# A planner rule that lets the attention's small tiled products of blocks 3 to 5 wait for company, and starts every block's attention 2 plan units earlier

## Chip, cores and metric

The kernel runs on one core of a Trainium2 chip. The metric is the device time in microseconds; before the change it is 610.1 us, the median of three runs (608.67 to 610.43).

## The reference, cut to what matters

A recurrent attention (state of 48 x 48 for each of 4 x 8 heads, 768 steps), then a dense layer of width 2048 with a gated activation, then a soft mixture of experts:

```python
cur = np.einsum('bhd,bhe->bhde', u[None] * kt, vt)
y[:, :, t] = np.einsum('bhd,bhde->bhe', rt, state + cur)
state = wt[:, :, :, None] * state + np.einsum('bhd,bhe->bhde', kt, vt)
...
h = x @ w_in
g = h * (1.0 / (1.0 + np.exp(-1.702 * h)))
return (g @ w_out).astype(np.float32)
...
slot_input = d.T @ x
h = np.maximum(slot_input[e] @ w1[e], 0.0)
return (c @ slot_out).astype(np.float32)
```

Here `d` and `c` are softmaxes of `x @ phi` over the tokens and over the slots.

## The kernel before

The 3072 tokens are cut into six blocks of 512 (128 time steps of each of the four batches). A block's attention is done in four units, one for a batch: units 0 to 3 belong to block 0, units 12 to 15 to block 3, units 20 to 23 to block 5. Block by block the dense layer and the first part of the mixture follow; the experts and the output come at the end.

One unit has these steps. VectorE scans the decays and scales `at` (L595, L609, L617). TensorE makes the products of keys and receptances inside a chunk of 64 steps into `aps` (L657; 16 small products of a 48-row by 64-column tile; the program's step `ta`). VectorE masks them into `st` (L669). TensorE then does two half units into `y` (L709 and L711, 64- and 48-column tiles over 112 or 128 rows; steps `h0` and `h1`). VectorE rescales the state after each (L716 into `vs`), adds the two parts (L719 into `nat`), TensorE transposes the result (L725 into `xps`), and ScalarE and VectorE split it into a high and a low part (`xth` L736, `xtl` L739). From block 2 on VectorE also transposes the keys (L694 to L698), in blocks 0 and 1 TensorE does it (L662).

The dense layer of a block takes 16 slices `f` of its width. For each, nine products of a full 128x128 array give `h` (L810), ScalarE applies the activation twice (`gh` L814, `g` L818), VectorE subtracts (`gl` L822), and nine more full products go into the three banks of `x2` (L830 to L832). Block 1 is done in two halves of 256 columns, the other blocks with 512. The mixture's share of a block is `lg` (L910), `ln` (L925), `en` (L954) and `pp` (L962) on TensorE, with 16 transposes into `x2g` on VectorE (L898) in blocks 1 to 3 and a copy `es` (L957). The raw weights of slice `f` come in by DMA (`raw`, L498) and are converted during block 0.

All of this is one list of steps. `Plan.order` plays it through with assumed costs, engine by engine: of the steps that are ready, the one with the lowest priority number goes next. The priority of a unit of block u is `begin(u) - AHEAD` plus a small step, so that attention of a block lies beside the dense layer of the block before it; that of slice `f` grows through the block's period of 82. The order that comes out is written down and each engine runs its own list strictly in that order.

A *small product* below is one of L657, L709 or L711 (and L910 and L962, which also use a part of the array's columns); a *stretch* is a run of small products with no full product between.

Of the kernel before, what the change touches and what calls it, by code (L numbers as in the profile page):

```python
# [52 lines left out]

SOON = "w0 r0 n0 w1 r1 v0 n1 v1 w2 r2 c0 n2 v2 w3 r3 c1 n3 v3 c2 c3"

FIRST, SECOND, PERIOD, LAG, AHEAD = 30.0, 150.0, 82.0, 4.2, 74.0
CONV0, CONVD, CONVL = 6.0, 4.0, 16.0
ATT0, ATTD = 3.0, 3.0
LAT = {"PE": 0.3, "ACT": 0.25, "DVE": 0.2, "POOL": 0.2, "DMA": 2.2, "X": 0.0}
SAME = {"PE": 0.0, "ACT": 0.2, "DVE": 0.12, "POOL": 0.1, "DMA": 2.2, "X": 0.0}  # L60
FROM = {"PE": 1.9, "ACT": 2.0, "DVE": 1.0, "POOL": 1.0, "DMA": 0.9}
MM = 0.238


def act(n):
# [3 lines left out]
def dve(n, rate=960):  # L69
    return 0.16 + n / rate  # L70
# [6 lines left out]
class Plan:  # L77
# [6 lines left out]

    def __init__(self, caps):
        self.caps, self.steps, self.users, self.tag = dict(caps), [], {}, {}

    def add(self, eng, cost, fn, need=(), pr=0.0, take=(), use=(), port=False):
        n = len(self.steps)
        opts = dict(eng) if isinstance(eng, dict) else {eng: cost}  # L90
        for tag, key in take:
            self.tag.setdefault(key, []).append(tag)
        keys = list(dict.fromkeys([k for _, k in take] + list(use)))
        for k in keys:
            self.users[k] = self.users.get(k, 0) + 1
        self.steps.append((opts, isinstance(eng, dict), fn, [x for x in need if x is not None], pr, [t for t, _ in take], keys, port))
        return n

    def order(self):
        steps, caps, left = self.steps, dict(self.caps), dict(self.users)  # L100
        wait = [len(s[3]) for s in steps]
        out = [[] for _ in steps]
        for i, s in enumerate(steps):
            for d in s[3]:
                out[d].append(i)
        ready, free, port = {}, {}, 0.0
        for s in steps:
            for e in s[0]:
                free[e] = FROM.get(e, 0.0)
                ready.setdefault(e, [])  # L110
        at, on = [0.0] * len(steps), [None] * len(steps)

        def enter(i):
            for e in steps[i][0]:
                ready[e].append(i)

        for i, s in enumerate(steps):
            if not wait[i]:
                enter(i)
        events, now, got = [(t, -1, -1) for t in sorted(FROM.values())], 0.0, []  # L120
        seq = 0
        self.log = []
        while len(got) < len(steps):
            moved = False
            for e in ready:
                if free[e] > now + 1e-9:
                    continue
                best = None
                for i in ready[e]:
                    s = steps[i]  # L130
                    if at[i] > now + 1e-9 or any(caps[t] < s[5].count(t) for t in s[5]):
                        continue
                    if (e == "POOL" or e == "DVE" and s[7]) and port > now + 1e-9:
                        continue
                    if best is None or (s[4], i) < (steps[best][4], best):
                        best = i
                if best is None:
                    continue
                s = steps[best]
                for x in s[0]:  # L140
                    ready[x].remove(best)
                on[best] = e
                for t in s[5]:
                    caps[t] -= 1
                got.append((best, e))
                self.log.append((now, s[0][e]))
                free[e] = now + s[0][e]
                if e == "POOL" or e == "DVE" and s[7]:
                    port = free[e]
                heapq.heappush(events, (free[e], seq, best))  # L150
                heapq.heappush(events, (free[e] + LAT[e], seq + 1, -1))
                seq += 2
                moved = True
            if moved:
                continue
            if not events:
                raise RuntimeError(f"plan stuck at {now}: {[(e, len(r)) for e, r in ready.items()]} {caps}")
            now, _, i = heapq.heappop(events)
            done = [i] if i >= 0 else []
            while events and events[0][0] <= now + 1e-9:  # L160
                k = heapq.heappop(events)[2]
                if k >= 0:
                    done.append(k)
            for i in done:
                e = on[i]
                for k in steps[i][6]:
                    left[k] -= 1
                    if not left[k]:
                        for t in self.tag.get(k, ()):
                            caps[t] += 1  # L170
                for j in out[i]:
                    wait[j] -= 1
                    at[j] = max(at[j], now + (SAME[e] if list(steps[j][0]) == [e] else LAT[e]))
                    heapq.heappush(events, (at[j], seq, -1))
                    seq += 1
                    if not wait[j]:
                        enter(j)
        self.span = now
        return got
# [185 lines left out]
def rwkv_moe_softmoe_kernel(tc: tile.TileContext, ark, aw, nat, vr, ub, wf, phi, w1, w2, r, k, v, w, ug, out):  # L365
# [16 lines left out]
    plan = Plan({"ps": 8, "h": 2, "a": 3, "g": 1, "gh": 2, "at": 2, "aw": 2, "nat": 2, "st": 2, "fl": 3, "q": 2,  # L382
                 "xt": 2, "xl": 2, "ind": 1, "raw": RAWB, "cq": CQB, "w": NF, "ew": NEW, "gl": 2})
# [167 lines left out]
    def unit_nodes(i):  # L551
        u, b = order[i]
# [11 lines left out]
        def pr(k):  # L564
            return base + step * k
# [134 lines left out]
        def half(p):  # L700
            vl, vh = VROW[p]
            ol, oh = RNG[p]
            yps = t_[ky0] if p else bank(ky0)
            sps = bank(ky1) if p and u < NU - 1 else yps
            k1 = (ROWS if u else CH) if p == 0 else P
            for h in range(NH):
                cols = slice(h * DH, (h + 1) * DH)
                rhs = v[0:k1, p, cols]
                pe.matmul(yps[vl:vh, cols], S[0][0:k1, p, h, 0:CH], rhs, start=True, stop=True)  # L709
                if p == 0 or u < NU - 1:  # L710
                    pe.matmul(sps[ol:oh, cols], S[0][0:k1, p, h, CH:ROWS], rhs, start=True, stop=True)  # L711
# [34 lines left out]
        few = u < UQ  # L746
        ln = N("DMA", 0.55 if few else 1.64, ld_n, pr=soon(f"n{i}", pr(1) - 5), take=[("nat", n_)])
        def psum(key):
            return [("ps", key), ("a", key)]
# [14 lines left out]
        ta = N("PE", 0.8 if four else 1.08, pa, [a1, r0], pr(2), take=[x for k in kap for x in psum(k)], use=[a_])  # L764
# [14 lines left out]
        h0 = N("PE", 1.06, lambda: half(0), [k0, rc[0], lv, h.get("s1")] + ke0, pr(4), take=psum(ky0), use=[s_])  # L779
        s0 = N("DVE", dve(DM), lambda: snew(0), [h0, h.get("h1")], pr(5), use=[ky0, f_])  # L780
        h1 = N("PE", 1.06, lambda: half(1), [s0, k1, rc[1], lv] + ke1 + (nst if u == 0 else []), pr(6), take=psum(ky1) if not last else [], use=[s_, ky0])
# [3 lines left out]
        xh = N("ACT", act(DM), xhi, [tx], pr(9), take=[("xt", kx), ("xl", kx)] if b == 0 else [], use=[kxp, kx])  # L785
        xl = N("DVE", dve(DM), xlo, [xh], pr(9), use=[kxp, kx])
        hist[i] = {"h0": h0, "h1": h1, "s1": s1}
        xt_ready[i] = xl
        att_all.extend([y1, xl] + ([s1] if s1 is not None else []))

# [3 lines left out]
    def mm_nodes(blk, f, lo, wd):  # L794
# [4 lines left out]
        cols = slice(lo, lo + wd)  # L799
        mm = MM * (wd + 18) / (T + 18)  # L800

# [209 lines left out]
    for u in range(NU):  # L1011
        for b in range(NB):
            unit_nodes(NB * u + b)
        for lo in range(0, T, WIDE[u]):
            for f in range(NF):
                mm_nodes(u, f, lo, WIDE[u])
        moe2_nodes(u)
# [189 lines left out]
    for i, wd in enumerate(PIECES):  # L1207
# [5 lines left out]
        for g in range(2):  # L1213
# [18 lines left out]
            for p in range(4):  # L1232
                keys = list(dict.fromkeys(f"w2_{a // (4 * DM)}" for a in at0[8 * p:8 * p + 8]))
                at = p0 + 0.5 + p if i and g else p0 - 1 + g + 0.1 * p
# [120 lines left out]
```

## Time and profile before

| what | value |
|---|---|
| median of three runs | 610.1 us (608.67 to 610.43) |
| the profiled execution | 612.51 us, of which the span of the instructions is 610.6 us |
| TensorE matmul busy | 571.3 us (94%) |
| VectorE busy | 446.8 us (73%) |
| ScalarE busy | 274.2 us (45%) |
| GpSimd busy | 57.5 us (9%) |
| full products of the dense layer, L810 and L830 to L832 | 204.8 + 121.6 and 124.9 + 120.9 + 120.8 us |
| small products L709, L711, L657 | 60.2, 49.1 and 23.0 us |

Busy times overlap on TensorE, since matmuls are pipelined and their ends are modelled; what a product costs is read from the distance between two starts.

### The profile page before, as it was taken

The numbers are of one execution on the slowest core, as the hardware profiler recorded it, in microseconds if no ns is written. First come the engines' busy times: TensorE is split into PE (matmuls) and PEld (weight loads), VectorE is DVE, ScalarE is ACT, GpSimd is POOL, SyncE is SP. The second block draws the span as 40 slices with busy tenths as digits, with TensorE's granted clock in tenths as the row PEclk, the third lists the DMA queues.
The fourth block names the chain that finished last, engine by engine and source line by source line (L and its number), as shares of the span: only waits on it lengthen the run. The fifth ranks groups of instructions, "written<-read, shape, count | busy, mean of one in ns | idle before, by whom it ended". The sixth has DMA issues, their size and how long they took to land.

```text
span 610.6 us, 12651 instructions
## 1 busy us (share of the span) xinstructions
PE 571.3 (94%) x5196; PEld 462.4 (76%) x5196; DVE 446.8 (73%) x867; ACT 274.2 (45%) x532; POOL 57.5 (9%) x67
## 2 busy tenths in 40 slices
PE   1977999999999999999999999999999999998992
PEld 1846788878899998778777778777788778886371
DVE  7698899998988898998989997699872342113221
ACT  3474687748634345344435242353342353324131
POOL 2000000000130111022111202110310000000000
PEclk9995899999999999999999999999999999999897
DMA  8946554724623233033421223230110296558738
GB/s 223 311 143 180 196 154 139 245 81 123 179 82 117 79 111 111 22 105 110 120 82 64 87 83 103 86 111 25 51 40 1 95 380 203 196 181 289 264 113 254
DMA packets 30276, 84.53 MB, mean 138 GB/s; under 512 B 3840, under 2 KB 13696, under 8 KB 30208
## 3 DMA queue, kind: packets, MB, share of 16 engines
q1 hardware_dynamic: 28624, 82.84, 42.2%
q8 instruction: 43, 0.70, 0.5%
q10 hardware_dynamic: 1584, 0.79, 0.5%
q14 instruction: 25, 0.20, 0.1%
HBM read 78.89 MB, written 4.72 MB: 137 GB/s over the span
## 4 chain that ended last, share of the span: by engine, by line
PE 80%; DVE 10%; DMA 5%; ACT 2%; issue 1%; SPq 0%; DVEq 0%; ACTq 0%
PE h L810 30%; PE x L830 11%; PE x L831 10%; PE x L832 10%; PE y L709 5%; DMA raw<-in_wf_dram 3%; DVE x2g L898 3%; PE aps L657 2%; DMA aw<-in_aw_dram 2%; PE eh L1180 2%; PE y L711 2%; PE so L1222 2%; PE xps L725 1%; PE fo L1263 1%; DVE at L617 1%
## 5 line engine op out<-in xcount | busy, mean ns | idle before, releaser
L810 PE MATMUL h<-xth,w 128*128 128x512 f32 (+1 forms) x672 | 204.8, 369 | 0.7 <-ACT xth L736 0.6
L814 ACT ACTIVATE ghgh<-h 128x512 fp32r<-128x512 f32 (+1 forms) x112 | 59.9, 535 | 196.5 <-PE h L810 152.7
L810 PEld LDWEIGHTS h<-xth,w 128*128 128x128 f32 x672 | 122.5, 190 | 21.5 <-ACT xth L736 1.2
L830 PE MATMUL x<-ghgh,w 128*128 128x512 f32 (+1 forms) x336 | 124.9, 372 | 0.0
L810 PE MATMUL h<-xtl,w 128*128 128x512 f32 (+1 forms) x336 | 121.6, 362 | 0.4 <-DVE xtl L739 0.4
L831 PE MATMUL x<-glgh,w 128*128 128x512 f32 (+1 forms) x336 | 120.9, 360 | 0.0
L832 PE MATMUL x<-ghgh,w 128*128 128x512 f32 (+1 forms) x336 | 120.8, 360 | 0.0
L822 DVE TENSOR_TENSOR glgh<-g,ghgh 128x512 fp32r<-128x512 f32 (+1 forms) x112 | 71.6, 639 | 59.0 <-ACT g L818 57.6
L830 PEld LDWEIGHTS x<-ghgh,w 128*128 128x128 f32 x336 | 63.4, 189 | 11.8 <-issue 1.7
L810 PEld LDWEIGHTS h<-xtl,w 128*128 128x128 f32 x336 | 63.9, 190 | 9.3 <-DVE xtl L739 1.1
L832 PEld LDWEIGHTS x<-ghgh,w 128*128 128x128 f32 x336 | 63.4, 189 | 9.6
L831 PEld LDWEIGHTS x<-glgh,w 128*128 128x128 f32 x336 | 63.5, 189 | 9.2 <-DVE glgh L822 0.4
L709 PEld LDWEIGHTS y<-vs,st 128*64 128x64 f32 (+2 forms) x768 | 53.4, 148 | 16.5 <-issue 8.0
L818 ACT ACTIVATE g<-h 128x512 f32<-128x512 f32 (+1 forms) x112 | 59.6, 532 | 9.0 <-DVE glgh L822 8.6
L709 PE MATMUL y<-vs,st 128*64 128x48 f32 (+2 forms) x768 | 60.2, 235 | 2.8 <-DVE vs L716 2.0
L711 PE MATMUL y<-vs,st 128*48 128x48 f32 (+2 forms) x704 | 49.1, 226 | 0.9 <-ACT st L679 0.8
L711 PEld LDWEIGHTS y<-vs,st 128*48 128x48 f32 (+2 forms) x704 | 43.1, 130 | 1.4 <-ACT st L679 1.2
L716 DVE TENSOR_TENSOR vs<-y,fl 48x384 f32<-48x384 f32 x44 | 24.5, 556 | 22.2 <-PE y L711 21.5
L669 DVE TENSOR_TENSOR st<-aps,mask 64x256 f32<-64x256 f32 (+1 forms) x80 | 37.9, 474 | 3.4 <-PE aps L657 2.0
L621 ACT ACTIVATE st<-at 48x512 f32<-48x512 f32 x44 | 27.6, 627 | 25.1 <-DVE at L617 13.4
L657 PE MATMUL aps<-at 48*64 48x64 f32 x768 | 23.0, 235 | 14.7 <-DVE at L617 14.7
L657 PEld LDWEIGHTS aps<-at 48*64 48x64 f32 x768 | 19.5, 145 | 21.0 <-DVE at L617 15.4
(159 smaller groups left out, 694.4 us busy)
## 6 DMA issues: line engine op xcount, KB each, us to landing
w<-in_w_dram SPq DMA_DIRECT2D x32, 768.0 KB, 6.0
at<-in_ark_dram SPq DMA_DIRECT2D x24, 512.0 KB, 4.2
raw<-in_wf_dram SPq DMA_DIRECT2D x16, 768.0 KB, 4.8
nat<-in_nat_dram SPq DMA_DIRECT2D x20, 576.0 KB, 3.7
aw<-in_aw_dram SPq DMA_DIRECT2D x24, 448.0 KB, 4.1
vs<-in_vr_dram SPq DMA_DIRECT2D x48, 96.0 KB, 2.5
out_dram<-ot SPq DMA_DIRECT2D x6, 512.0 KB, 6.8
nat<-in_nat_dram SPq DMA_DIRECT2D x4, 192.0 KB, 4.9
```

The source lines that it names most:

```text
L621: ac.activation(S[0][lo:hi, p, :, 0:CH], t_[a_][lo:hi, 0], AF.Copy)
L657: pe.matmul(ab[p if four else 0][vl:vh, col:col + CH], t_[a_][lo:hi, 1, 4 * g + h], t_[a_][lo:hi, 0, 4 * g + h], start=True, stop=True)
L669: ve.tensor_tensor(S[0][vl:vh, p, n * g:n * g + n, 0:CH], t_[kap[p if four else 0]][al:ah, 0:n * CH].rearrange("p (h t) -> p h t", h=n), m ...
L709: pe.matmul(yps[vl:vh, cols], S[0][0:k1, p, h, 0:CH], rhs, start=True, stop=True)
L711: pe.matmul(sps[ol:oh, cols], S[0][0:k1, p, h, CH:ROWS], rhs, start=True, stop=True)
L810: pe.matmul(h[:, :wd], a, b, start=(k == 0), stop=(k == len(seq) - 1))
L814: ac.activation(t_[kgh][0], t_[kh][:, :wd], AF.Gelu_apprx_sigmoid)
L818: ac.activation(t_[kg], t_[kh][:, :wd], AF.Gelu_apprx_sigmoid)
L822: ve.tensor_tensor(gl, t_[kg], gh.bitcast(F32), op=ALU.subtract)
L830: pe.matmul(o, whi, gh, start=(f == 0), stop=False)
L831: pe.matmul(o, whi, gl, start=False, stop=False)
L832: pe.matmul(o, wlo, gh, start=False, stop=(f == NF - 1))
```

## The change

`AHEAD` goes from 74 to 76, which moves the priority of every unit from block 1 on. The steps `ta`, `h0` and `h1` of blocks 3 to 5 (units 12 to 23) are put into a set `tiled`. When the planner picks TensorE's next step, such a step gets 50 off its priority number if the step just placed was of the set too; otherwise, if fewer than two of the ready steps are of the set, it gets 500 on top until it has been ready for 8 plan units. The planner also adds 0.2 to its own cost of a step of the set that follows one outside it. No step is added or removed.

```diff
-FIRST, SECOND, PERIOD, LAG, AHEAD = 30.0, 150.0, 82.0, 4.2, 74.0
+FIRST, SECOND, PERIOD, LAG, AHEAD = 30.0, 150.0, 82.0, 4.2, 76.0
...
+SWITCH, HOLD, GROUP = 0.2, 8.0, 2
...
+                    can.append(i)
+                few = sum(i in self.tiled for i in can) < 2
+                rank = {i: steps[i][4] for i in can}
+                for i in can if e == "PE" else []:
+                    if i in self.tiled:
+                        rank[i] += -50.0 if tiled else 500.0 if few and now < at[i] + HOLD else 0.0
+                for i in can:
+                    s = steps[i]
...
-                    if best is None or (s[4], i) < (steps[best][4], best):
+                    if best is None or (rank[i], i) < (rank[best], best):
...
+                if e == "PE":
+                    free[e] += SWITCH if best in self.tiled and not tiled else 0.0
+                    tiled = best in self.tiled
...
+        if u > GROUP:
+            plan.tiled.update((ta, h0, h1))
```

In the changed program line numbers are 14 higher from the planner on, and 16 higher from the dense layer on.

**TensorE at the turn from block 3 to block 4.** `y0_19`/`y1_19` is unit 19's second half unit (its last row here), `aps20` and `y0_20` are unit 20's, `h4_0` opens block 4. Before:

```order
L711 MATMUL y1_19_4516<-vs3_95,st1_97 48x48
L810 MATMUL h3_15_0_4533<-xth3_3110,w15_1215 128x512
...
L725 MATMUL xps19_4548<-ident_78,nat19_4171 128x128 x3
L657 MATMUL aps20_0_4557<-at20_4231 64x64
...
L810 MATMUL h4_0_0_4584<-xth4_3995,w0_237 128x512
```

With the change:

```order
L725 MATMUL y0_19_4464<-vs3_95,st1_97 48x48
L671 MATMUL aps20_0_4481<-at20_4137 64x64
...
L846 MATMUL x2_3_0_3841<-ghgh3_13_0_4448,w13_1095 128x512
...
L725 MATMUL y1_19_4525<-vs3_95,st1_97 48x48
L723 MATMUL y0_20_4547<-vs0_92,st0_96 64x48
...
L826 MATMUL h3_15_0_4568<-xth3_3189,w15_1209 128x512
...
L739 MATMUL xps19_4581<-ident_78,nat19_4217 128x128 x3
L846 MATMUL x2_3_0_3841<-ghgh3_14_0_4542,w14_1149 128x512
...
L846 MATMUL x2_3_0_3841<-ghgh3_15_0_4585,w15_1209 128x512
...
L826 MATMUL h4_0_0_4631<-xth4_3923,w0_237 128x512
```

Unit 20's `aps` now stands right behind unit 19's first half, its first half right behind unit 19's second, and between the transposes of unit 19 and block 4's first product there are two groups of full products (and unit 20's second half) where there was only `aps20`.

**VectorE behind unit 9's second half unit**, in the second half of block 1 (the first row of each reads `y1_9`). Before:

```order
L716 TENSOR_TENSOR vs1_93<-y1_9_2199,fl9_1977 48x384
L822 TENSOR_TENSOR glgh1_15_0_2191<-g1_15_0_2197,ghgh1_15_0_2190 128x256
L719 TENSOR_TENSOR nat9_1798<-y0_9_2149,nat9_1798 128x384
L609 SCALAR_TENSOR_TENSOR aw10_1761<-aw10_1761,ind_91 112x512
L822 TENSOR_TENSOR glgh1_0_256_2232<-g1_0_256_2245,ghgh1_0_256_2231 128x256
L617 TENSOR_TENSOR at10_1836<-at10_1836,aw10_1761 112x1024
L739 TENSOR_TENSOR xtl2_1960<-xps9_2248,xth2_1959 128x3x128
L822 TENSOR_TENSOR glgh1_1_256_2267<-g1_1_256_2279,ghgh1_1_256_2266 128x256
L694 STREAM_TRANSPOSE st0_96<-at10_1836 32x8x32 x2
```

With the change:

```order
L733 TENSOR_TENSOR nat9_1778<-y0_9_2146,nat9_1778 128x384
L623 SCALAR_TENSOR_TENSOR aw10_1845<-aw10_1845,ind_91 112x512
L608 MEMSET ind_91 112x8
L609 SCALAR_TENSOR_TENSOR aw11_2093<-aw11_2093,ind_91 112x512
L838 TENSOR_TENSOR glgh1_0_256_2247<-g1_0_256_2264,ghgh1_0_256_2246 128x256
L753 TENSOR_TENSOR xtl2_2054<-xps9_2242,xth2_2053 128x3x128
L631 TENSOR_TENSOR at10_1891<-at10_1891,aw10_1845 112x1024
L614 TENSOR_TENSOR fl11_2308<-aw11_2093 112x8
L708 STREAM_TRANSPOSE st0_96<-at10_1891 32x8x32 x2
L710 STREAM_TRANSPOSE st0_96<-at10_1891 32x8x32 x2
L708 STREAM_TRANSPOSE st0_96<-at10_1891 32x8x32 x2
L838 TENSOR_TENSOR glgh1_1_256_2277<-g1_1_256_2280,ghgh1_1_256_2276 128x256
```

The subtraction `gl` of slice 1 now stands behind a scan of unit 11 and six transposes of unit 10 that came after it or elsewhere before; the `gl` of slice 15 no longer stands in this piece.

**SyncE's DMA issues in block 0.** `vs0` is the load of unit 8's values, which waits for both half units of unit 4. Before:

```order
L498 DMA raw13_1036<-in_wf_dram 128x2x768
L572 DMA aw7_1056<-in_aw_dram 112x1024
L498 DMA raw14_1112<-in_wf_dram 128x2x768
L589 DMA vs0_92<-in_vr_dram 64x384
L590 DMA vs0_92<-in_vr_dram 64x384
L498 DMA raw15_1166<-in_wf_dram 128x2x768
```

With the change:

```order
L512 DMA raw13_1043<-in_wf_dram 128x2x768
L603 DMA vs0_92<-in_vr_dram 64x384
L604 DMA vs0_92<-in_vr_dram 64x384
L512 DMA raw14_1110<-in_wf_dram 128x2x768
L586 DMA aw7_1134<-in_aw_dram 112x1024
L512 DMA raw15_1153<-in_wf_dram 128x2x768
```

The load of the values moved ahead of that of the weights of slice 14, and `aw7` behind it.

## Rows read from the trace of the kernel before

**Rows 1.** The page's busy times, and VectorE's busy tenths in 40 slices of the span.
```profile
PE 571.3 (94%) x5196; PEld 462.4 (76%) x5196; DVE 446.8 (73%) x867; ACT 274.2 (45%) x532; POOL 57.5 (9%) x67
DVE  7698899998988898998989997699872342113221
```

**Rows 2.** The page's chain by engine; pieces of the chain: start us, us, what.
```profile
PE 80%; DVE 10%; DMA 5%; ACT 2%; issue 1%; SPq 0%; DVEq 0%; ACTq 0%
177.41 1.08 PE h L810 x9
...
200.48 0.62 PE aps L657 x32
...
509.61 2.04 PE h L810 x9
```

**Rows 3.** Timeline of TensorE: start us, us, engine line op names shapes xcount [idle before <-releaser].
```profile
335.74 0.39 PE L832 MATMUL x<-ghgh,w 128*128 128x512 f32 x1
336.06 0.26 PE L709 MATMUL y<-vs,st 112*64 112x48 f32 x1
...
336.91 0.28 PE L709 MATMUL y<-vs,st 112*64 112x48 f32 x2
337.12 0.50 PE L830 MATMUL x<-ghgh,w 128*128 128x512 f32 x1
337.46 0.39 PE L831 MATMUL x<-glgh,w 128*128 128x512 f32 x1
...
339.39 0.26 PE L709 MATMUL y<-vs,st 128*64 128x48 f32 x1
```

**Rows 4.** Timeline of TensorE: `aps` followed by `y` and by a transpose.
```profile
109.41 1.15 PE L657 MATMUL aps<-at 48*64 48x64 f32 x32
110.48 0.26 PE L709 MATMUL y<-vs,st 112*64 112x48 f32 x1
...
137.31 1.15 PE L657 MATMUL aps<-at 48*64 48x64 f32 x32
138.39 0.60 PE L662 MATMUL kps<-ident,at 112*128 112x112 f32 x4
```

**Rows 5.** Timeline of TensorE: waits at three turns of blocks.
```profile
155.00 0.85 PE L962 MATMUL pp<-x2g,es 128*32 128x385 f32 x8 [0.52 <-DVE es L957]
...
333.01 0.85 PE L962 MATMUL pp<-x2g,es 128*32 128x385 f32 x8 [0.29 <-DVE x2g L898]
...
398.93 0.49 PE L725 MATMUL xps<-ident,nat 128*128 128x128 f32 x3
399.35 0.69 PE L657 MATMUL aps<-at 48*64 48x64 f32 x32
400.15 0.49 PE L810 MATMUL h<-xth,w 128*128 128x512 f32 x1
401.03 0.50 PE L810 MATMUL h<-xtl,w 128*128 128x512 f32 x1 [0.38 <-DVE xtl L739]
```

**Rows 6.** Timeline of VectorE: behind unit 9, and single rows of other stretches.
```profile
192.46 0.55 DVE L716 TENSOR_TENSOR vs<-y,fl 48x384 f32<-48x384 f32 x1 [1.48 <-PE y L711]
193.04 0.42 DVE L822 TENSOR_TENSOR glgh<-g,ghgh 128x256 fp32r<-128x256 f32 x1
...
196.90 0.42 DVE L822 TENSOR_TENSOR glgh<-g,ghgh 128x256 fp32r<-128x256 f32 x1
197.35 0.88 DVE L694 STREAM_TRANSPOSE st<-at 32x256 f32<-32x256 f32 x2
...
382.49 0.16 DVE L600 TENSOR_TENSOR fl<-aw 112x8 f32<-112x8 f32 x1
...
399.20 0.07 DVE L594 MEMSET ind<- 112x8 f32 x1
399.30 1.22 DVE L595 TENSOR_TENSOR_SCAN aw<-aw,ind 112x512 f32<-112x512 f32 x1
...
404.28 2.00 DVE L617 TENSOR_TENSOR at<-at,aw 112x1024 f32<-112x1024 f32 x1
```

More of the change, by code (lines that the diff above doesn't have):

```diff
@@ L86, in __init__ @@
         self.caps, self.steps, self.users, self.tag = dict(caps), [], {}, {}
+        self.tiled = set()
     def add(self, eng, cost, fn, need=(), pr=0.0, take=(), use=(), port=False):
@@ L121, in order @@
         seq = 0
-        self.log = []
+        self.log, tiled = [], False
         while len(got) < len(steps):
@@ L127, in order @@
                     continue
-                best = None
+                best, can = None, []
                 for i in ready[e]:
```

## Prediction

> **What bounds the kernel now.** I read the busy times and the chain first. TensorE is busy 94% of the span, and the chain of waits that ends last runs through it for 80%, through VectorE for 10% [rows 1, 2]. VectorE's slices stand at 8 and 9 tenths for the first two thirds of the span and then fall to 1 to 4 [rows 1]. So TensorE sets the pace, and until about 420 us VectorE is close enough behind to make it wait at single points. What this change can bring is therefore of two kinds: time that TensorE loses at each turn between full and small products, and waits on VectorE that come or go.
>
> The price of a turn is in the timeline [rows 3]. Nine full products of 512 columns take 2.04 us [rows 2], 0.23 a product. The first product of a half unit starts 0.32 us after the last full one instead of 0.23: 0.09 to go in. Inside, starts follow each other every 0.03 us (31st at 336.91, first at 336.06), although 64- and 48-column tiles alternate; from the 32nd to the next full product it is about 0.15, so 0.12 more to get out. The second full product then comes 0.34 after the first instead of 0.23, and the group of nine that lies between two half units takes 337.12 to 339.39, 2.27 instead of 2.04: without the 0.09 of the next entry that is 0.14 to get going again. One stretch of small products costs 0.09 + 0.12 + 0.14 = 0.35 us beyond its own work.
>
> **The change, part by part.** No product is added or taken away, so everything lies in the order.
>
> *Fewer stretches.* I counted them in the two orders, from block 1's first `aps` to block 5's first product; before and behind that, TensorE's order is the same. Before there are 64 stretches, with the change 56. Before, 4 neighbours are of unlike shape (`aps5` ahead of a half unit, and three `pp` ahead of one). With the change 12 are neighbours: 4 times a half unit follows another (units 15/16, 17/18, 19/20, 21/22), 6 times `aps` follows a half unit, and once each `lg` and `pp` lie beside one.
> - Two half units side by side: the trace has no such pair at full speed. Bounds: 0.23, if the way out is paid between them all the same, and 0.35, if nothing is. Since no break shows inside a half unit where its tiles alternate [rows 3], I take 0.35: 4 x 0.35 = 1.40 us.
> - Unlike shapes side by side: `aps` takes 1.08 us up to the start of a half unit and 1.08 up to a transpose that uses the whole width [rows 4]. The way out is paid whatever follows; entry and restart, 0.09 + 0.14 = 0.23, are saved. Bounds: nothing, and the whole 0.35. With 0.23, 8 new ones less the 4 given up give 4 x 0.23 = 0.92.
>
> Together 2.3 us. The Trainium skill, page "TensorEngine Tiling (Array Packing)", section "Tiling Modes", says that changing the tiling mode, and not just the tile, drains TensorE. That speaks against the six places where `aps` (48 rows) follows a half unit (112 or 128 rows), since the mode changes there as well. If each change cost half of the 0.35, an unlike pair would save 0.18 and the sum would be 1.40 + 4 x 0.18 = 2.1 us; the rows on `aps` agree that the drain stays.
>
> *Waits that go.* Three waits of TensorE on VectorE stand at turns of blocks [rows 5]. At 400.15 block 4's first product begins 1.2 us after unit 19's transposes, and its second, which reads `xtl`, comes 0.88 later instead of 0.34: 0.54 lost. The new order puts two groups of full products and a half unit there, over 5 us. `pp` of block 0 waits 0.52 for `es`, because it stood straight behind `en`; now a group of nine of 256 columns and a third of another lie between, 1.4 us [rows 2]. `pp` of block 2 waits 0.29 for the last `x2g` transpose; it gets one more group of nine ahead of it, 2.04. Sum 1.35 us, with nothing of it left if the VectorE work ahead is on time there.
>
> *A wait that comes.* The 2 units of `AHEAD` pull unit 11's scan ahead of a subtraction that TensorE needs in block 1. Before, VectorE's piece from the rescaling behind unit 9 to the `gl` of slice 1 ran from 192.46 to 197.32, 4.86 us without a gap [rows 6]. Now it lacks one narrow `gl` (0.35 after overlap) and holds also a memset and a scan (1.24), `fl` (0.1) and three pairs of transposes (0.88 each, 2.65): 8.5 us, from 0.1 after unit 9's second half. TensorE, in that time, has six narrow groups of 1.08 [rows 2], the restart 0.14, three transposes at about 0.3 (0.42 where a small product comes next [rows 5]), the entry 0.09 and `aps10` at 0.62 [rows 2]: 7.6. The second product of the next group, 0.12 on, reads `gl`. So TensorE waits 8.6 - 7.7 = 0.9 us. Lower bound 0, if VectorE gets there early. Upper bound: `at`'s scaling took 2.00 in one place instead of about 1.2 [rows 6]; if that 0.8 fell on all three long operations of the piece, 0.9 + 2.4 = 3.3.
>
> *What is moved at no cost.* A half unit held back for up to 8 plan units delays its unit, but the next user of its state is the same batch's unit one block on; what needs it soonest is the first product of the next block. There unit 23's transposes have one group of nine ahead of block 5's first product, 2.04 us, before and after; if that cover went, the wait would be of the kind of the 0.54 above. Transposes of unit 21 come only 1.06 us after its second half; L719 needs 0.55 of that and VectorE has nothing else queued that is ready. On SyncE the load of unit 8's values now stands ahead of the weights of slice 14, and waits for unit 4, which ends before the raw buffer comes free; should it be late, slice 14 is late by as much, and its product stands some 2 us later than before. `aw7` behind it is needed a unit later. GpSimd (9% busy) has some multiplications in another order, with units of slack. ScalarE keeps its work and its table loads.
>
> **Sum.** -2.32 - 1.35 + 0.9 = -2.8 us. Against the profiled execution (612.5 us, span 610.6 and 1.9 around it) that is 609.7; that execution lies 2.4 over the median, so from 610.1 I predict **607.3 us**.
>
> **Rivals.**
> - *More comes back.* Unlike neighbours save the whole 0.35 (12 x 0.35 - 4 x 0.35 = 2.8) and unit 9's piece is met without a wait: -2.8 - 1.35 = -4.15, 605.9 us. For it: VectorE had idle time of 1.48 just before that piece [rows 6]. Against: `aps` shows its way out.
> - *The rule does only half of what it says.* The drain is the whole price, so that unlike neighbours save nothing: 1.40 + 1.35 - 0.9 = 1.85, 608.25 us. For it: [rows 4]; against: the 0.14 of restart lies in the full products.
> - *Waits only move.* Unit 9's piece costs the upper bound of 3.3: -2.32 - 1.35 + 3.3 = -0.4, 609.7 us. For it: VectorE at 8 to 9 tenths there [rows 1].
> - *Slower: VectorE's pile in block 1 repeats.* With scans and scalings that run slow beside GpSimd, the late subtraction makes unit 10's masks late too, and the same 3.3 is paid again one unit on: -3.7 + 6.6 = +2.9, 613.0 us. It decides from 5.5 us of such waits in all, since 3.7 are gained and 1.8 is the band. For it: L617's 2.00. Against: in this part of the old trace such a piece ran without a gap.
>
> **How the numbers follow.** About 0.3% (1.8 us) is what a measurement of this kernel can tell from no change. Chances: the forecast 0.45, more comes back 0.18, half a rule 0.10, waits only move 0.18, slower 0.09. Faster by over 0.3% (under 608.3): 0.45 + 0.18 + 0.04 of the half rule, which lies on the border, 0.67. Within: 0.06 + 0.18 = 0.24. Slower: 0.09. The range goes from 605.0, the better case with the 0.9 that medians of three runs differ by, to 610.4, which holds the moved waits with less than that margin; outside lie the slower case and some 0.1 of the tails.
>
> **What would show it.** Right: about 56 stretches; side by side half units whose 64 products run on at 0.03 with no 0.15 between; no idle time ahead of block 4's first products, `pp` of block 0 and `pp` of block 2; a wait near 0.9 us of the 256-column products on `glgh` some 8 us behind unit 9's second half. Wrong: a break of 0.15 between two half units; full products after a long stretch that are slower than 0.34; or new idle time of TensorE over 3 us in blocks 1 to 4, on `glgh`, `vs` or `st`, which would mean that VectorE, not the turns, sets the pace there.

## The result: slower, and the profile after

| kernel | median | ratio to the kernel before, 95% interval |
|---|---|---|
| before | 610.3 us (4 runs) | |
| changed | 617.8 us (616.6 to 618.7, 4 runs) | 1.012 [1.010, 1.014] |

The prediction was 607.3 us, 605.0 to 610.4. The time is outside the range and on the other side. The profiled execution of the changed kernel took 617.22 us (span 615.4), that of before 612.51 (span 610.6).

The page of the changed kernel: busy times, VectorE's and the granted TensorE clock's tenths in 40 slices, and the chain by engine.

```profile
PE 570.3 (93%) x5196; PEld 464.9 (76%) x5196; DVE 445.3 (72%) x868; ACT 273.8 (44%) x531; POOL 56.6 (9%) x67
DVE  8788898998989993899969989879981341212331
PEclk9985899999999999799999999999999999999996
PE 76%; DVE 13%; DMA 5%; issue 2%; ACT 1%; SPq 0%; POOL 0%; DVEq 0%; ACTq 0%
```

Against [rows 1, 2], the busy times differ by 2.5 us at most. TensorE has lost 4% of the chain to VectorE and "issue", and VectorE has one slice at 3 where it stood at 8. The clock's row dips to 7 in the slice behind it. So the loss is one hole at about 240 us. TensorE's timeline there (start us, us, what, [idle before <-releaser]):

```profile
241.07 0.26 PE L723 MATMUL y<-vs,st 112*64 112x48 f32 x1
...
241.92 0.28 PE L723 MATMUL y<-vs,st 112*64 112x48 f32 x2
249.85 1.13 PE L671 MATMUL aps<-at 48*64 48x64 f32 x32 [7.65 <-issue]
250.92 0.79 PE L826 MATMUL h<-xth,w 128*128 128x512 f32 x1
...
254.62 0.40 PE L846 MATMUL x<-ghgh,w 128*128 128x512 f32 x1
```

Behind unit 12's first half TensorE waits 7.65 us for `aps13`, which the rule has pulled right behind that half. Then `aps13` takes 1.07 us to the next start where [rows 2] have 0.62, and the group of nine takes 3.70 where one that restarts takes 2.18 (2.04 and 0.14). Together 7.65 + 0.45 + 1.52 = 9.6 us. The busy times by stretch (stretch, length, busy of PE, PEld, DVE, ACT, POOL, granted clock, DMA share, GB/s) say why the products behind the hole are slow:

```profile
225.00:241.00 16.00, 16.00 (x166) 14.82 (x164) 11.68 (x26) 5.82 (x16) 1.32 (x2) 1.00 0.38 112
241.00:249.80 8.80, 1.21 (x34) 1.01 (x32) 1.70 (x3) 1.05 (x4) 3.07 (x3) 0.67 0.00 0
249.80:255.00 5.20, 5.14 (x43) 4.25 (x44) 5.04 (x9) 2.36 (x4) 0.64 (x1) 0.57 0.32 91
255.00:262.00 7.00, 7.00 (x33) 5.76 (x32) 6.84 (x13) 1.68 (x3) 0.00 (x0) 1.00 0.00 0
```

The granted clock was 1.00 up to the hole, fell within it, stood at 0.57 for the first 5 us of work behind it (most of that at the lower of its two levels, 1.2 GHz) and came back.

The profile names no releaser for this wait (it says "issue"), so who held `aps13` up has to be read from the other engines. VectorE's timeline, then GpSimd's, then SyncE's issue of unit 13's `nat` (0.7 us earlier than before the change), all of the changed kernel:

```profile
236.85 1.22 DVE L623 TENSOR_TENSOR_SCAN aw<-aw,ind 112x512 f32<-112x512 f32 x1
248.07 0.55 DVE L658 TENSOR_REDUCE q<-nat 128x8 f32<-128x384 f32 x1 [10.00 <-POOL nat L640]
248.54 1.22 DVE L631 TENSOR_TENSOR at<-at,aw 112x1024 f32<-112x1024 f32 x1
```
```profile
230.62 0.94 POOL L661 TENSOR_TENSOR nat<-nat,q 128x384 f32<-128x384 f32 x1 [12.63 <-DVE q L658]
238.53 0.38 POOL L1046 PARTITION_ALL_REDUCE pool<-pool  x1 [6.96 <-issue]
245.98 0.98 POOL L639 TENSOR_TENSOR nat<-nat 128x384 f32<-128x384 f32 x1 [7.08 <-issue]
247.04 0.99 POOL L640 TENSOR_TENSOR nat<-nat,ubt 128x384 f32<-128x384 f32 x1
```
```profile
231.95 0.33 SPq L600 DMA_DIRECT2D nat<-in_nat_dram  x1
```

Read from the end: `aps13` needs `at13`'s scaling (L631), and starts 0.1 us after it ends. In VectorE's strict order the reduction `q13` (L658) stands just ahead of it, and that waits 10.00 us for GpSimd's two multiplications of `nat13`. GpSimd is late because it does a dummy all-reduce of `pool0` between two multiplications, a 0.38 us operation with 6.96 us of "issue" ahead of it and 7.08 behind it: 14 us in which GpSimd is not "busy". The program's instruction list has an extra GpSimd instruction ahead of each of these two pauses, which has no row in the profile; by its place it is the change of GpSimd's code library and back. No run separates that change from the all-reduce itself. The kernel before has both too. Its GpSimd and VectorE:

```profile
222.84 0.83 POOL L647 TENSOR_TENSOR nat<-nat,q 128x384 f32<-128x384 f32 x1 [4.26 <-DVE q L644]
229.55 0.38 POOL L1030 PARTITION_ALL_REDUCE pool<-pool  x1 [5.88 <-issue]
237.59 1.02 POOL L625 TENSOR_TENSOR nat<-nat 128x384 f32<-128x384 f32 x1 [7.67 <-DMA nat<-in_nat_dram]
238.69 1.01 POOL L626 TENSOR_TENSOR nat<-nat,ubt 128x384 f32<-128x384 f32 x1
```
```profile
254.25 0.50 DVE L644 TENSOR_REDUCE q<-nat 128x8 f32<-128x384 f32 x1
...
260.63 1.22 DVE L617 TENSOR_TENSOR at<-at,aw 112x1024 f32<-112x1024 f32 x1
```

There `nat13` was ready at 239.7, and `q13` came 14.5 us later. In the changed kernel GpSimd does the all-reduce 9 us later (238.53 for 229.55), and VectorE comes to `q13` 16 us earlier (it is free for it at 238.07, for 254.25). GpSimd's own order is the same here in both kernels: `nat12` by `q12` (L647, now L661), the all-reduce, `nat13`. Both shifts come out of VectorE's order: `q12`, for which the multiplication ahead of the all-reduce waits, now stands 8 us later (the multiplication starts at 230.62 for 222.84), and `q13` earlier.

Beside this hole the changed kernel did most of what the prediction said. A pair of half units, and the three places of [rows 5] (`pp` of block 0, `pp` of block 2, block 4's first product):

```profile
321.30 0.26 PE L723 MATMUL y<-vs,st 128*64 128x48 f32 x1
...
322.15 0.29 PE L723 MATMUL y<-vs,st 128*64 128x48 f32 x4
322.26 0.21 PE L725 MATMUL y<-vs,st 112*48 112x48 f32 x1
...
323.19 0.50 PE L826 MATMUL h<-xth,w 128*128 128x512 f32 x1
```
```profile
152.23 0.85 PE L978 MATMUL pp<-x2g,es 128*32 128x385 f32 x8
...
347.14 0.85 PE L978 MATMUL pp<-x2g,es 128*32 128x385 f32 x8
...
412.93 0.39 PE L826 MATMUL h<-xth,w 128*128 128x512 f32 x1
413.16 0.39 PE L826 MATMUL h<-xtl,w 128*128 128x512 f32 x1
```

The 64 products run through with no break where one half ends, 1.89 us to the next full product. None of the three places waits any more. The wait that comes, behind unit 9, on TensorE and on VectorE (answering to [rows 6]; in the section on the change, the changed order of this piece begins one row too late, behind the `vs` shown here, and its first row reads `y0_9`):

```profile
199.06 0.38 PE L846 MATMUL x<-ghgh,w 128*128 128x256 f32 x1
200.48 0.39 PE L847 MATMUL x<-glgh,w 128*128 128x256 f32 x1 [1.04 <-DVE glgh L838]
```
```profile
191.57 0.55 DVE L730 TENSOR_TENSOR vs<-y,fl 48x384 f32<-48x384 f32 x1 [0.38 <-PE y L725]
...
199.97 0.46 DVE L838 TENSOR_TENSOR glgh<-g,ghgh 128x256 fp32r<-128x256 f32 x1
```

From `vs` to the end of `gl` it is 8.86 us (8.5 predicted), and the wait is 1.04 (0.9 predicted).

### The profile page after: what moved, and what is told of

It reads as the page before. It is cut to its first block, busy times and chain, and to the rows that moved or that the text cites. A ratio compares the mean times of both kernels' runs of the same rounds, so it can differ in the third digit from the quotient of the medians.

```text
span 615.4 us, 12646 instructions
## 1 busy us (share of the span) xinstructions
PE 570.3 (93%) x5196; PEld 464.9 (76%) x5196; DVE 445.3 (72%) x868; ACT 273.8 (44%) x531; POOL 56.6 (9%) x67
## 4 chain that ended last, share of the span: by engine, by line
PE 76%; DVE 13%; DMA 5%; issue 2%; ACT 1%; SPq 0%; POOL 0%; DVEq 0%; ACTq 0%
PE h L826 29%; PE x L846 10%; PE x L847 10%; PE x L848 10%; PE y L723 4%; DVE x2g L914 3%; DMA raw<-in_wf_dram 3%; PE aps L671 3%; PE eh L1196 2%; PE so L1238 2%; PE y L725 2%; DVE glgh L838 1%; DMA aw<-in_aw_dram 1%; PE xps L739 1%; DVE at L631 1%
## 5 line engine op out<-in xcount | busy, mean ns | idle before, releaser
L826 PEld LDWEIGHTS h<-xth,w 128*128 128x128 f32 x672 | 123.8, 192 | 21.9 <-ACT xth L750 1.0
L838 DVE TENSOR_TENSOR glgh<-g,ghgh 128x512 fp32r<-128x512 f32 (+1 forms) x112 | 70.1, 626 | 69.4 <-ACT g L834 67.8
```

The lines of the kernel that those rows point to most:

```text
L826: pe.matmul(h[:, :wd], a, b, start=(k == 0), stop=(k == len(seq) - 1))
L838: ve.tensor_tensor(gl, t_[kg], gh.bitcast(F32), op=ALU.subtract)
```

## The experiments

The theory is named "library": the all-reduce takes GpSimd away for 14 us, and VectorE's strict order hands that on to TensorE. Beside each median below stands the length of the **middle** in that kernel's trace, from the first product of slice 8 in block 0 to block 5's `lg`. It leaves out the start and the end, which together differ by up to 4 us between the profiled executions (143.0 to 147.1). Before it is 464.07 us (93.36 to 557.43), with the change 470.85 (92.58 to 563.43).

**e1_no_dummy: the all-reduce taken out.**

```diff
-    N("POOL", 0.57, lambda: gp.partition_all_reduce(pool0[:, 1:2], pool0[:, 0:1], ...), [xt_ready[NB * 3 - 1]], 0)
+    N("POOL", 0.57, lambda: None, [xt_ready[NB * 3 - 1]], 0)
```

> The changed kernel without GpSimd's dummy all-reduce of pool0 (L1046); its place in the plan stays, so the order on TensorE and VectorE is that of the changed kernel. Nothing of the output depends on it. Theory 'library': the all-reduce makes GpSimd idle for 6.96 and 7.08 us around it, q13 on VectorE waits for nat13 behind that, at13's scaling stands behind q13 and aps13 behind the scaling. Without it the wait of 7.65 us ahead of aps13 goes, and with it the slow products behind (0.44 + 1.5): 617.8 - 9.6 = 608.2 us, 607.4 to 609.2. Rival 'transfer': nat13's load is late by itself and the idle time beside the all-reduce is only GpSimd waiting for it: the wait stays and the time is 617 to 618.5. Rival 'pile on VectorE': something else that VectorE has queued there is long: half of it stays, over 611.

Measured: 609.4 us, ratio 0.9976 [0.9950, 1.0002]; middle 462.77. That is 8.4 us less than the changed kernel in the medians and 8.1 in the middle. TensorE, GpSimd and VectorE of this kernel:

```profile
243.00 0.69 PE L671 MATMUL aps<-at 48*64 48x64 f32 x32
243.63 0.50 PE L826 MATMUL h<-xth,w 128*128 128x512 f32 x1
...
255.40 0.50 PE L847 MATMUL x<-glgh,w 128*128 128x512 f32 x1 [1.05 <-DVE glgh L838]
```
```profile
237.38 1.29 POOL L639 TENSOR_TENSOR nat<-nat 128x384 f32<-128x384 f32 x1 [4.95 <-DMA nat<-in_nat_dram]
```
```profile
240.60 0.55 DVE L658 TENSOR_REDUCE q<-nat 128x8 f32<-128x384 f32 x1 [0.84 <-POOL nat L640]
241.07 1.22 DVE L631 TENSOR_TENSOR at<-at,aw 112x1024 f32<-112x1024 f32 x1
```

The wait of 7.65 us is gone, and `aps13` takes 0.63 again. "Transfer" falls: `nat13` does land only at 237.4, but GpSimd uses it then and not at 246. "Pile on VectorE" falls as well, since the time is under 611. It lies 1.2 above the expected 608.2, just over the range: a wait of 1.05 us on `glgh` comes 12 us later (5.63 us for a group of 18 that otherwise takes 4.08, so 1.55), which the hole had hidden.

**e2_ahead_only: AHEAD = 76, the rule for no block.**

```diff
-SWITCH, HOLD, GROUP = 0.2, 8.0, 2
+SWITCH, HOLD, GROUP = 0.2, 8.0, 9
```

> The changed kernel with the rule for no block (GROUP 9), so AHEAD = 76 alone. aps13 stands some 8 us later in TensorE's order than with the rule. Theory 'library, met through AHEAD': VectorE still has q13 ahead of glgh2_0_0, which TensorE's products of slice 0 of block 2 read at about 241.4 us in the changed kernel's time; q13 ends at about 248.5, glgh2_0_0 at about 249.2. The wait is only moved from aps13 to these products: about 7.8 us and the slow products behind it, so 610.3 + 9.5 + 1.0 (the wait behind unit 9) - 0.5 (pp of block 0) = about 620, over 617 in any case. Rival 'the pull': it is the rule's -50 that set aps13 ahead of its operands, AHEAD alone is harmless: 610.3 + 1.0 - 0.5 = 610.8, 610 to 612.

Measured: 625.8 us, ratio 1.024 [1.020, 1.028]; middle 478.58. VectorE and TensorE:

```profile
247.33 0.55 DVE L658 TENSOR_REDUCE q<-nat 128x8 f32<-128x384 f32 x1 [10.06 <-POOL nat L640]
247.80 0.68 DVE L838 TENSOR_TENSOR glgh<-g,ghgh 128x512 fp32r<-128x512 f32 x1
```
```profile
248.53 0.80 PE L847 MATMUL x<-glgh,w 128*128 128x512 f32 x1 [8.03 <-DVE glgh L838]
```

The same 10 us on VectorE, and 8.03 us on TensorE, now ahead of slice 0's products. The rule's pull on `aps13` is not the cause; it only decides which product meets the wait. The time is 6 us over the estimate; e7 says what is in it.

**e3_rule_only: the rule with AHEAD = 74.**

```diff
-FIRST, SECOND, PERIOD, LAG, AHEAD = 30.0, 150.0, 82.0, 4.2, 76.0
+FIRST, SECOND, PERIOD, LAG, AHEAD = 30.0, 150.0, 82.0, 4.2, 74.0
```

> The changed kernel with AHEAD = 74, so the rule alone. 52 stretches of small products for 64 before: 5 half units beside another and 11 unlike neighbours for 4. Theory 'library, met through AHEAD': q13 stands late on VectorE, as before the change, no such wait comes. Stretches 5 x 0.46 + 7 x 0.23 = 3.9 us (0.46 is what a pair saves in the changed kernel's trace), the waits of block 4's first product and of pp of block 2 gone (0.54 + 0.29): 610.3 - 4.7 = 605.6, 604.8 to 607.5. Rival 'the pull': aps pulled forward wait for their scaling: 612 or more.

Measured: 611.6 us, ratio 1.0009 [0.9984, 1.0034]; middle 466.65. No wait on GpSimd, as expected, but no gain either: a miss by 6 us. The time is near the 612 of "the pull", but no `aps` waits. In its place TensorE waits at five points between 315 and 494 us, four times for VectorE, once for ScalarE's `xth`; of these only the last was there before, with 0.39 us. The first, on TensorE:

```profile
315.31 0.49 PE L846 MATMUL x<-ghgh,w 128*128 128x512 f32 x1
317.18 0.50 PE L847 MATMUL x<-glgh,w 128*128 128x512 f32 x1 [1.38 <-DVE glgh L838]
...
318.41 0.63 PE L848 MATMUL x<-ghgh,w 128*128 128x512 f32 x1
```
```profile
318.00:320.50 2.50, 2.50 (x7) 1.97 (x6) 1.41 (x4) 1.30 (x3) 1.00 (x1) 0.50 0.92 299
```

The group takes 4.81 us instead of 2.04: 1.38 of wait, then products 0.43 apart instead of 0.23, at a granted clock of 0.50 (the second fence, a row by stretch as above). Ahead of that `glgh` VectorE had a scan, a scaling and ten transposes, 309.6 to 316.4, with one other `glgh` between. That is only part of it: ScalarE gave the `g` that this `gl` reads at 315.52, after standing 3.18 us for the same scaling, so VectorE's pile explains 0.9 of the 1.38. The other waits are 0.51, 0.79, 0.74 and 1.38. Reading only TensorE's order told what the stretches save, not what VectorE and ScalarE then owe.

**e5_before_no_dummy: the kernel before without the all-reduce** (the edit of e1).

> The kernel before without the dummy all-reduce; order on TensorE and VectorE unchanged, output unaffected. Theory 'library': before the change nobody waited for GpSimd behind it (q13 came 15 us after nat13's products), so 610.3, within 0.6 of the kernel before. Rival: the pass through the other library already cost something before, or the dummy prepares the all-reduce at the end: over 0.6 faster, or slower.

Measured: 610.3 us, ratio 0.9990 [0.9967, 1.0013]; middle 464.16 against 464.07. Before the change the 14 us cost nothing that can be measured.

**e7_ahead_no_dummy: e2 without the all-reduce** (both edits).

> AHEAD = 76 alone (as e2_ahead_only), without the dummy all-reduce; the orders of TensorE and VectorE are those of e2_ahead_only. Theory 'library, met through AHEAD': the group of 18 products on glgh2_0_0 that took 13.20 us there takes about 4.1 (the wait of 8.03 and its slow products go), and the products behind it, 2.3 us slow in e2_ahead_only, run at full speed: 625.8 - 9.1 - 2.3 = 614.4, 611 to 615.5. What stays over the kernel before is the wait behind unit 9 (1.1) and small ones on VectorE. Rival 'AHEAD alone costs it': 623 or more.

Measured: 615.9 us, ratio 1.009 [1.006, 1.013]; middle 467.95. The hole is worth 9.9 us here; the estimate is met within 1.5, just over its upper end. But `AHEAD` alone still costs 5.3 us with nobody waiting for GpSimd, where e2's estimate had 0.5 (1.0 less 0.5). The trace has waits of 1.09 (unit 9), 0.55 (on ScalarE's `g`), 0.86 (`glgh`), 0.37 twice (the `xtl` wait that [rows 5] have with 0.38, now at two turns) and 1.38 (on VectorE near the end). With the rule on top (e1) the time is 6.5 less and the middle 5.2: the rule saves stretches (the order of e7 has 64, as before the change) and puts full products in between that cover the `xtl` waits. That these two and the 1.38 (0.39 in e1) make up the whole difference is argued, not tested.

**e8_q13_later: the all-reduce kept, `q13` moved.** TensorE's order is untouched. The multiplication on GpSimd that reads `q13` moves with it.

```diff
-        for i, e in self.order():
+        got = self.order()
+        put = [g for g in got if g[0] in unit["q"]]
+        got = [g for g in got if g[0] not in unit["q"]]
+        k = [g[0] for g in got].index(unit["h0"])
+        got[k:k] = put
+        for i, e in got:
...
-        hist[i] = {"h0": h0, "h1": h1, "s1": s1}
+        hist[i] = {"h0": h0, "h1": h1, "s1": s1, "q": (qs, qm)}
...
-    plan.emit()
+    plan.emit(hist[13])
```

> The changed kernel with the dummy all-reduce where it was, and unit 13's reduction q13 on VectorE and its multiplication on GpSimd moved in the order to just ahead of unit 13's first half on TensorE. TensorE's order is that of the changed kernel; on VectorE q13 alone moves, from ahead of at13's scaling to some 40 instructions behind it. Theory 'library by way of VectorE's strict order': GpSimd is away as long as before, nobody stands behind q13, the wait of 7.65 us goes as in e1_no_dummy: 608 to 610.5. Rival 'shared path': while GpSimd changes its library, VectorE's own work beside it is held up: the wait stays, 615 to 618.

Measured: 608.4 us, ratio 0.9969 [0.9945, 0.9993]; middle 462.05. GpSimd is away as long as before, and VectorE goes on:

```profile
245.11 1.00 POOL L639 TENSOR_TENSOR nat<-nat 128x384 f32<-128x384 f32 x1 [7.24 <-issue]
```
```profile
235.16 1.22 DVE L623 TENSOR_TENSOR_SCAN aw<-aw,ind 112x512 f32<-112x512 f32 x1
236.41 1.23 DVE L631 TENSOR_TENSOR at<-at,aw 112x1024 f32<-112x1024 f32 x1
...
240.21 0.69 DVE L838 TENSOR_TENSOR glgh<-g,ghgh 128x512 fp32r<-128x512 f32 x1
```
```profile
240.44 0.69 PE L671 MATMUL aps<-at 48*64 48x64 f32 x32
```

The scaling follows the scan at once, `aps13` starts without a wait, and the 1.05 us of e1 are gone too, presumably since VectorE does not stand for `q13` at all (e11, with `q13` in the same place, still has 0.34 there). "Shared path" falls. The whole loss hung on two things together, the all-reduce and the place of one reduction in VectorE's order: taking away either (e1, e8) ends it.

**e4_planner_told: a cost of 15 for the all-reduce in the plan.**

```diff
-    N("POOL", 0.57, lambda: gp.partition_all_reduce(pool0[:, 1:2], ...
+    N("POOL", 15.0, lambda: gp.partition_all_reduce(pool0[:, 1:2], ...
```

> The changed kernel with the dummy all-reduce at a cost of 15 in the plan instead of 0.57, so that the planner knows how long GpSimd is away. The planner then puts unit 12's two halves side by side ahead of it and aps13 six groups later, but q13 and q14 still stand on VectorE ahead of the last glgh of block 1. GpSimd reaches the all-reduce at about 231.6 as in the changed kernel, so q13 starts at about 248 and q14 at about 250; TensorE comes to the products on that glgh at about 244.5. Theory 'library by way of VectorE's strict order': a wait of about 6.5 us there, with some 1.5 of slow products: 610.3 + 8 + 1.0 - 1.4 - 3.5 = about 614.5, 612.5 to 617. Rival 'the missing cost was all': 606 to 608.

Measured: 622.8 us, ratio 1.022 [1.017, 1.027]; middle 476.21. The expected wait is there, 6.99 us on the last `glgh` of block 1, behind `q13` and `q14`. The estimate is 8 us short: beside it stand waits of 0.67 inside unit 12's pair and 1.29 ahead of its transposes, 2.70 ahead of `pp` of block 1 (behind x2g transposes), and full products at a granted clock of 0.50 for 5 us behind the 6.99 and for 3 us behind the 2.70.

```profile
250.61 0.58 PE L847 MATMUL x<-glgh,w 128*128 128x256 f32 x1 [6.99 <-DVE glgh L838]
```

The planner had the hole in its own plan: played through, that plan has the all-reduce from 228.8 to 243.8 plan units, this `gl` only at 250.1, and TensorE empty from 239.4 to 250.7. `Plan.order` lets no step marked `port`, as `gl` is, start while GpSimd is busy, so 15 units for the all-reduce shut `gl` out as well. On the chip they do not: in e8 a `gl` runs in its usual 0.69 us while GpSimd is away. So e4 told the planner of a busy time where the chip has an absence, and what a rightly told cost would bring stays untested.

**e9_hold4_no_dummy: e1 with a shorter hold.**

```diff
-SWITCH, HOLD, GROUP = 0.2, 8.0, 2
+SWITCH, HOLD, GROUP = 0.2, 4.0, 2
```

> AHEAD = 76 and the rule with HOLD = 4 instead of 8, without the dummy all-reduce: a small product waits less long for a second stretch. 53 stretches of small products, 5 half units side by side, 10 unlike neighbours (4 and 9 in e1_no_dummy). Stretches 0.7 us better than e1_no_dummy. Theory 'stretches pay what they measured, VectorE gives back': 609.4 - 0.7 = 608.7 if VectorE's waits are those of e1_no_dummy, 607 to 609 where HOLD's shorter delay takes some away; over 610 if the closer half units make VectorE pile up as in e3_rule_only.

Measured: 611.1 us, ratio 1.0012 [0.9978, 1.0045]; middle 464.21. The second outcome: waits on VectorE of 1.32, 1.09 and 1.09 us at 254, 338 and 421 us take back the stretches. (Counted as in the prediction it has 54 stretches and 9 unlike neighbours.)

**e10_q13_and_glgh: e8, and the `gl` behind unit 9 moved.**

Here `emit` takes any number of such moves, `hist[1, 1, 256]` is the step of that `gl`, and `r0` the scaling of `at`.

```diff
-    plan.emit(hist[13])
+    plan.emit((hist[13]["q"], hist[13]["h0"]), ([hist[1, 1, 256]], hist[10]["r0"]))
```

> e8_q13_later with one more move on VectorE: the 256-column glgh of slice 1 in block 1, on which TensorE waits 1.23 us behind unit 9 (the wait that the prediction put at 0.9), goes ahead of at10's scaling and its transposes; its operand g is there at 194.1, the scaling starts at 194.06, so it takes 0.4 from aps10, which has 1.2 to spare. TensorE's order stays. Theory: that wait goes and the group behind unit 9 takes 1.1 instead of 2.66 us: 608.4 - 1.5 = 606.9, 605.8 to 607.9. Rival: aps10 or the next glgh is late by as much instead: 608.4.

Measured: 607.4 us, ratio 0.9948 [0.9928, 0.9967]; middle 461.13. TensorE behind unit 9:

```profile
199.97 0.39 PE L846 MATMUL x<-ghgh,w 128*128 128x256 f32 x1
200.19 0.28 PE L847 MATMUL x<-glgh,w 128*128 128x256 f32 x1
```

The wait is gone; 0.29 of it comes back ahead of the next group, which takes 1.72 us instead of 1.08. This is the lowest median of the versions and faster than both kernels; its interval overlaps those of e8 and e11. Against e8 it gains 1.0 of the 1.5 expected (0.9 in the middle).

**e11_both_no_dummy: e10 without the all-reduce** (the edit of e1).

> e10_q13_and_glgh without the dummy all-reduce. With q13 out of the way nobody waits for GpSimd behind it, so theory 'library by way of VectorE's strict order' expects no difference: within 0.6 of e10_q13_and_glgh, 606.9. Rival 'GpSimd's absence still costs something', by nat13 and nat14 late on GpSimd: over 0.6 faster.

Measured: 608.1 us, ratio 0.9953 [0.9927, 0.9978]; middle 461.35. That is 0.7 above e10, a little outside the expected 0.6 but on the other side from the rival, and the middles differ by 0.2: with `q13` out of the way GpSimd's absence costs nothing that can be measured.

## Why the prediction was wrong

The step that failed is one sentence: "GpSimd (9% busy) has some multiplications in another order, with units of slack." It took the busy share for the engine's availability and "units of slack" from the order of before, and did not look who stands behind the reader of those multiplications on VectorE. Nor was it GpSimd's order that mattered: that differs at units 8, 17 and 21 alone, while the hole came from two reductions that changed their places on VectorE. What the runs showed in place of the sentence is a wait of 10.00 us of VectorE for GpSimd, and 7.65 us of TensorE behind it. GpSimd's 14 us around L1030 are not in its busy time, but its timeline shows them as idle time of 5.88 ahead and 7.67 behind. The rivals had VectorE late by its own work only; that VectorE could stand still for another engine was in none of them. Its own test, "new idle time of TensorE over 3 us", did hit, but on an operand that it had not listed (`at`), and not because VectorE's own work set the pace. The Trainium skill, page "GPSIMD Engine Reference", section "2.1 Instruction dispatch", says that the first call of a newly loaded kernel costs some 6 us that no instruction in the profile shows, and that one should budget for it. The traces agree as to the pause ahead of the all-reduce, 5.88 us before the change and 6.96 with it. They have a second pause that the section does not speak of, 7.08 us ahead of the ordinary multiplication behind it (before the change, 7.67 there ended with a transfer).

Point by point:
- **Fewer stretches, -2.32: right, a little low.** A pair takes 1.89 us where two lone half units take 2 x 1.06 = 2.12, and saves one entry and restart besides (0.09 + 0.14): 0.46 each, where 0.35 was taken, the upper bound of the prediction. An unlike pair pays its way out (a half unit ahead of `aps` takes 1.06, `aps` then 0.62): 0.23, as taken. 4 x 0.46 + 4 x 0.23 = 2.76. Small waits at new neighbours (0.30 ahead of `ln`, 0.24 ahead of `pp` in e8) take some of it back.
- **Waits that go, -1.35: right**, all three.
- **A wait that comes, +0.9: right in place and in the length of the wait** (1.04 to 1.23), but with the slow product behind it the group of 256 columns takes 2.48 to 2.66 us, where one behind `aps10` took 1.18 before, so the price is 1.3 to 1.5.
- **Sum.** With the hole, -2.76 - 1.35 + 1.3 + 9.6 = +6.8 for the middle; measured +6.78 (a small wait of 0.31 ahead of `ln` is left out, so the last tenth is luck). Without the hole (e8) -2.76 - 1.35 + 1.5 + 0.5 (the two small waits) = -2.1; measured -2.02, where the forecast had -2.8. That e10 comes out at 607.4 beside the forecast of 607.3 is luck: it has no longer the wait behind unit 9, which the forecast counted. As made the change costs 7.5.
- **The two parts.** By e2, e3 and e7 neither is worth anything alone. `AHEAD` = 76 alone costs 15.1 us, 9.9 of it by the hole. The rule alone changes nothing that can be measured. The prediction had only counted their sum.

## What to carry to other kernels

An engine's busy share does not say when it is available: look through its timeline for idle time put down to "issue", and treat those stretches as work with a place in the order. When an order moves, take each strictly ordered engine and ask of every instruction that now stands earlier whether its operand from another engine does too; one early reader holds up all that is behind it. And look at what else a cost does in a planner before giving it one: charged as busy time (e4), the all-reduce also shut out subtractions that the chip does beside it, and the wait moved and hardly shrank (6.99 for 7.65), while moving two VectorE instructions by hand (e10) brought the gain.

## What the runs showed of the hardware

- GpSimd's all-reduce between multiplications took 0.38 us of busy time (0.89 in e8, 0.91 in e10) and 13.6 to 14.4 us of idle time around it, in all seven traces that have it: 6.96 + 7.08 with the change, 7.04 + 7.12 in e2, 7.16 + 7.16 in e4, 7.11 + 7.24 in e8, 7.09 + 7.17 in e10. In the kernel before (5.88 + 7.67) and in e3 (5.84 + 7.82) the second part is not put down to "issue".
- A hole of TensorE can cost more than its length. After 7.65 us the granted clock was 0.57 for 5 us, and 2.0 us more were lost; after only 1.38 us of waiting (e3), behind transposes and `aps`, full products also ran 0.43 apart instead of 0.23 for at least 2.5 us, at a granted clock of 0.50; after the 1.05 us of e1 it stayed at 1.00 and none was slow.
- Small products of 128 and of 112 rows follow each other with no break: at the seam of two half units the last four of the one take 0.11 up to the first of the other, 0.03 each, and 64 products take 1.89 us. The program gives both the same tile size, 128 x 64. `aps`, with 64 x 64, is not met so: the half unit ahead of it takes its 1.06 us, as ahead of a full product.
